# A second Strassen level inside one of the seven products of a cross-network kernel

## The chip, the cores and the metric

The kernel runs on one core of one Trainium2 chip. The metric is the device time of one execution in microseconds (us). Every kernel time below is a median of fast runs; the repeats of one kernel agree within 0.3%. Profile figures are of one execution. The traces kept for runs 1 to 4 (the first four experiments) are of another execution of the same kernel than the one quoted here; figures marked "kept trace" were counted there. The engines are named as in the profile: PE is TensorE (matmuls), PEld its weight loads, DVE is VectorE, ACT is ScalarE, SP issues the transfers.

## The reference

```python
B, Din, L = 16384, 1024, 6          # x0 [B, Din], ws [L, Din, Din], bs [L, Din], all bf16
def reference(x0, ws, bs):
    x = x0
    for l in range(L):
        proj = jnp.einsum('bd,de->be', x, ws[l]) + bs[l]
        x = x0 * proj + x
    return x
```

Each of the six layers multiplies x by a 1024x1024 matrix, and layer l+1 needs the whole result of layer l.

## The kernel before

x is kept transposed in SBUF (features on partitions). 1024 rows of the batch, called a pair, are taken through all six layers, then the next 1024: 16 pairs x 6 layers = 96 rounds, called layers here. Within a layer, one Strassen (Winograd) step cuts the product into blocks of 512: seven products of 512x512x512 instead of eight. A product is 16 matmuls of 512 columns. Block (eh, n) is output half eh (512 features) of batch half n (512 rows).

The T's are differences of blocks of x, made by DVE. The weight combinations are made by DVE in the first pair and then reloaded from memory. PSUM holds two tiles `pA` and two tiles `px`, each of two banks.

```python
rhs_of = {1: blk(xsrc, 0, 0), 2: blk(xsrc, 1, 0), 3: blk(xsrc, 1, 1),
          4: Ts[4][:], 5: Ts[1][:], 6: Ts[2][:], 7: Ts[3][:]}

def product(pid, pts, start):                    # 16 matmuls
    ...                                          # (weight tile wt, cut)
    for m in range(KH):
        for k in range(KH):
            nc.tensor.matmul(pts[m // 2][:, m % 2, :], lhsT=wt[:, k, m * P:(m + 1) * P], rhs=rhs[:, k, :],
                             start=(start and k == 0), stop=(k == KH - 1), **kw)

def evac(pts, bias_eh=None, dst=None):           # ScalarE: PSUM -> SBUF, bf16
    ...                                          # two 1024-element copies, or four 512-element ones with a bias

def final(Cb, eh, n):                            # VectorE: x_new = x0 * c + x, block by block
    c = Cb[:, :, n, :]
    nc.vector.tensor_tensor(out=c, in0=c, in1=blk(x0T, eh, n), op=MULT)
    ...                                          # (last pair, cut)
    nc.vector.tensor_tensor(out=blk(xst, eh, n), in0=c, in1=blk(xsrc, eh, n), op=ADD)

# (PSUM allocation and the first pair's weight combinations cut)
product(1, pA, True);   P1s = evac(pA)
product(5, pX, True);   P5s = evac(pX)
product(3, pX, False);  S53 = evac(pX, bias_eh=0)
product(2, pX2, True);  P2s = evac(pX2, bias_eh=0)
nc.vector.tensor_tensor(out=C1[:, :, 0, :], in0=P1s, in1=P2s, op=ADD)
final(C1, 0, 0)                                  # block (0,0): what the next layer's product 1 reads
product(6, pA, False);  U2s = evac(pA)
nc.vector.tensor_tensor(out=C1[:, :, 1, :], in0=U2s, in1=S53, op=ADD)
final(C1, 0, 1)
...                                              # T1 of the next layer
product(7, pA, False);  U3s = evac(pA, bias_eh=1)
nc.vector.tensor_tensor(out=C2[:, :, 1, :], in0=U3s, in1=P5s, op=ADD)
final(C2, 1, 1)
product(4, pA, False);  evac(pA, bias_eh=1, dst=C2[:, :, 0, :])
final(C2, 1, 0)
...                                              # T2, T3, T4 of the next layer
```

The order of the products is 1, 5, 3, 2, 6, 7, 4. A scheduler fixes the order on each engine at build time; it may depart from the order in which the code is written.

## Time and profile before

| | before |
|---|---|
| time | 2354.6 us (2354.53 to 2354.66, 2 runs) |
| PE / DVE / ACT busy | 98% / 73% / 66% |
| matmuls in the program | 10752, all of 512 columns |

The page's first part gives busy time and share of the span, its fourth part the chain of work that ended last, by engine:

```profile
PE 2312.4 (98%) x10537; PEld 1052.7 (45%) x10752; DVE 1708.6 (73%) x1464; ACT 1556.7 (66%) x2113; POOL 1.2 (0%) x5
...
PE 96%; DVE 1%; DMA 1%; issue 1%; SPq 1%; ACT 0%; another core or an unknown queue 0%; DVEq 0%
```

Matmuls overlap (the trace gives one a mean duration of 379 ns), so a busy PE is not yet a PE at its limit. What counts is the time from one start to the next. In the trace of the kernel before it is 216 ns (median of all neighbours), and 10752 x 0.216 = 2322 us of the 2353 us span. (2% of the matmul records are missing, so the page counts 10537.) The table of waits (who waited for whom: us in total, times, longest) agrees. PE is in none of its large lines; other engines wait for PE or for each other:

```profile
DVE cb L235 <- ACT ev L208: 594.2, 96, 7.9
ACT ev L205 <- PE pa L196: 230.8, 368, 14.2
ACT ev L208 <- PE px L196: 193.3, 369, 0.8
```

The timeline of one layer (start, duration, what, count, and in brackets idle time before it) shows when block (0,0) is ready:

```profile
1214.45 3.62 PE L196 MATMUL pa<-T_9079,wp 128*128 128x512 bf16 x16
...
1215.95 1.23 DVE L235 TENSOR_TENSOR cb<-ev 128x2048 bf16<-128x2048 bf16 x1 [6.43 <-ACT ev L208]
...
1217.21 1.22 DVE L214 TENSOR_TENSOR cb<-cb,x0T 128x2048 bf16<-128x2048 bf16 x1
...
1218.54 1.23 DVE L223 TENSOR_TENSOR xst<-cb,xst 128x2048 bf16<-128x2048 bf16 x1
...
1223.34 1.27 ACT L208 ACTIVATE cb<-pa,b_all 128x512 bf16<-128x512 f32 x2 [0.51 <-ACT ev L208]
...
1224.81 0.38 PE L196 MATMUL pa<-xst,wp 128*128 128x512 bf16 x1
```

Add, multiply, add for block (0,0) end at 1218.54 + 1.23 = 1219.77. The next layer's product 1 (the last line) starts at 1224.81. Block (0,0) is five microseconds early, and PE does not stop.

### The profile page before, as it was taken

To read this page: it belongs to the slowest core of one execution; us is meant where nothing else is said; L and a number is where in the kernel's file an instruction comes from. 1 tells how busy PE (TensorE), PEld (TensorE's weight loads), DVE (VectorE), ACT (ScalarE), POOL (GpSimd) and SP (SyncE) were. 2 spreads that over 40 slices of the span, in tenths; PEclk is the share of its full clock that TensorE was granted. 3 is DMA by queue.
4 is the path that set the end of the run, shared out by engine and by line. 5 is a ranking of instruction groups with operands and counts; after the bars stand their busy time and mean duration, and the time that the engine had idled before them with its cause. 6 is when DMAs were issued, how large, how long until landed. Compare 5 with 4: busy or idle time off the path is not lost.

```text
span 2352.8 us, 27562 instructions
## 1 busy us (share of the span) xinstructions
PE 2312.4 (98%) x10537; PEld 1052.7 (45%) x10752; DVE 1708.6 (73%) x1464; ACT 1556.7 (66%) x2113; POOL 1.2 (0%) x5
## 2 busy tenths in 40 slices
PE   7999999999999999999999999999999999999997
PEld 3444444444444444444444444444444444444443
DVE  5977767676777767676776767677776767777675
ACT  4666666666666666666666666666666666666665
POOL 0000000000000000000000000000000000000000
PEclk9999999999999999999999999999999999999998
DMA  7769485584956849568494774947749476594843
GB/s 226 203 210 256 152 216 196 161 253 154 228 184 171 241 154 240 171 177 235 153 259 153 178 233 152 259 152 190 221 152 260 153 198 214 155 257 152 226 153 86
DMA packets 599987, 457.96 MB, mean 195 GB/s; under 512 B 398128, under 2 KB 550704, under 8 KB 599856
## 3 DMA queue, kind: packets, MB, share of 16 engines
q1 hardware_dynamic: 599856, 456.20, 67.0%
q8 instruction: 85, 1.39, 0.2%
q14 instruction: 46, 0.38, 0.1%
HBM read 342.88 MB, written 46.14 MB: 165 GB/s over the span
## 4 chain that ended last, share of the span: by engine, by line
PE 96%; DVE 1%; DMA 1%; issue 1%; SPq 1%; ACT 0%; another core or an unknown queue 0%; DVEq 0%
PE pa L196 54%; PE px L196 42%; SPq L145 1%; DMA w_313<-in_ws_dram 0%; DMA wp<-in_ws_dram 0%; DVE cb L214 0%; DVE xst L219 0%; DVE xst L223 0%; ACT ev L208 0%; DVE cb L241 0%; DVE cb L250 0%; DVE cb L235 0%; DVE wp L128 0%; DVE T_247 L93 0%; DVE T_811 L93 0%
## 5 line engine op out<-in xcount | busy, mean ns | idle before, releaser
L196 PEld LDWEIGHTS <-wp 128*128 128x128 bf16 x10752 | 1052.7, 98 | 1283.8 <-issue 12.7
L208 ACT ACTIVATE ev<-px,b_all 128x512 bf16<-128x512 f32 x768 | 486.3, 684 | 201.3 <-PE px L196 193.3
L196 PE MATMUL px<-xst,wp 128*128 128x512 bf16 x2510 | 562.5, 379 | 2.7
L235 DVE TENSOR_TENSOR cb<-ev 128x2048 bf16<-128x2048 bf16 x96 | 117.6, 1225 | 594.2 <-ACT ev L208 594.2
L205 ACT CAST ev<-pa 128x1024 bf16<-128x1024 f32 x384 | 388.6, 1012 | 240.2 <-PE pa L196 230.8
L214 DVE TENSOR_TENSOR cb<-cb,x0T 128x2048 bf16<-128x2048 bf16 x384 | 467.8, 1221 | 6.3
L223 DVE TENSOR_TENSOR xst<-cb,xst 128x2048 bf16<-128x2048 bf16 x316 | 385.0, 1222 | 14.5
L208 ACT ACTIVATE ev<-pa,b_all 128x512 bf16<-128x512 f32 x384 | 243.1, 684 | 112.9 <-PE pa L196 108.2
L208 ACT ACTIVATE cb<-pa,b_all 128x512 bf16<-128x512 f32 x384 | 243.1, 684 | 88.4 <-ACT ev L208 48.4
L196 PE MATMUL pa<-xst,wp 128*128 128x512 bf16 x1254 | 287.3, 379 | 1.3
L205 ACT CAST ev<-px 128x1024 bf16<-128x1024 f32 x192 | 194.3, 1012 | 138.1 <-PE px L196 133.1
L241 DVE TENSOR_TENSOR cb<-ev 128x2048 bf16<-128x2048 bf16 x96 | 117.0, 1219 | 0.0
L250 DVE TENSOR_TENSOR cb<-ev 128x2048 bf16<-128x2048 bf16 x96 | 117.0, 1218 | 0.0
L196 PE MATMUL px<-x0T,wp 128*128 128x512 bf16 x501 | 112.4, 379 | 0.5
L223 DVE TENSOR_TENSOR xst<-cb,x0T 128x2048 bf16<-128x2048 bf16 x64 | 78.3, 1223 | 1.5
L196 PE MATMUL pa<-x0T,wp 128*128 128x512 bf16 x251 | 60.2, 391 | 12.9 <-DMA x0T<-in_x_dram 12.6
L130 DVE TENSOR_TENSOR wp<-wp 128x2048 bf16<-128x2048 bf16 x6 | 7.3, 1219 | 2.1 <-DMA wp<-in_ws_dram 2.1
L128 DVE TENSOR_TENSOR wp<-wp 128x2048 bf16<-128x2048 bf16 x6 | 7.3, 1219 | 0.0
L126 DVE TENSOR_TENSOR wp<-w_90,wp 128x2048 bf16<-128x2048 bf16 x1 | 1.2, 1226 | 8.2 <-DMA wp<-in_ws_dram 8.2
L93 DVE TENSOR_TENSOR T_111<-x0T 128x2048 bf16<-128x2048 bf16 x1 | 1.2, 1226 | 5.7 <-DMA x0T<-in_x_dram 5.7
L219 DVE TENSOR_TENSOR xst<-cb,xst 128x2048 bf16<-128x2048 bf16 x4 | 4.9, 1225 | 0.1
L196 PE MATMUL px<-T_247,wp 128*128 128x512 bf16 x16 | 3.6, 378 | 0.3 <-DVE T_247 L93 0.3
(783 smaller groups left out, 1858.9 us busy)
## 6 DMA issues: line engine op xcount, KB each, us to landing
wp<-Lc SPq DMA_DIRECT2D x360, 512.0 KB, 3.4
wp<-in_ws_dram SPq DMA_DIRECT2D x288, 512.0 KB, 3.7
out_dram<-x0T SPq DMA_DIRECT2D x30, 1024.0 KB, 9.8
Lc<-wp SPq DMA_DIRECT2D x24, 512.0 KB, 3.1
out_dram<-xoS SPq DMA_DIRECT2D x4, 512.0 KB, 4.7
w_90<-in_ws_dram SPq DMA_DIRECT2D x1, 512.0 KB, 4.7
x0T<-in_x_dram SPq DMA_TRANSPOSE x32, 7.3
w_130<-in_ws_dram SPq DMA_DIRECT2D x1, 512.0 KB, 5.0
```

What stands on the lines that cost most here:

```text
L128: nc.vector.tensor_tensor(out=t_[:], in0=wtiles[(0, l, 5)][:], in1=W11[:], op=SUB)
L130: nc.vector.tensor_tensor(out=t_[:], in0=W21[:], in1=wtiles[(0, l, 6)][:], op=SUB)
L145: nc.sync.dma_start_transpose(out=x0T_next[:, n], in_=x0[n * NB:(n + 1) * NB, :])
L196: nc.tensor.matmul(pts[m // 2][:, m % 2, :], lhsT=wt[:, k, m * P:(m + 1) * P], rhs=rhs[:, k, :], start=(start and k == 0), stop=(k == KH - ...
L205: nc.scalar.copy(out=dst[:, 2 * h:2 * h + 2, :], in_=pts[h][:])
L208: nc.scalar.activation(out=dst[:, m, :], in_=pts[m // 2][:, m % 2, :], func=IDENT, bias=bias_col(bias_eh, m), scale=1.0)
L214: nc.vector.tensor_tensor(out=c, in0=c, in1=blk(x0T, eh, n), op=MULT)
L219: nc.vector.tensor_tensor(out=xo_last["xfin"][:, eh, n].rearrange("r j k p -> r k j p"), in0=v4(c), in1=v4(blk(xsrc, eh, n)), op=ADD)
L223: nc.vector.tensor_tensor(out=blk(xst, eh, n), in0=c, in1=blk(xsrc, eh, n), op=ADD)
L235: nc.vector.tensor_tensor(out=C1[:, :, 0, :], in0=P1s, in1=P2s, op=ADD)
L241: nc.vector.tensor_tensor(out=C1[:, :, 1, :], in0=U2s, in1=S53, op=ADD)
L250: nc.vector.tensor_tensor(out=C2[:, :, 1, :], in0=U3s, in1=P5s, op=ADD)
```

## The change

Product 2, W21*B21, is itself cut into blocks of 256 and done with seven inner products, each of four matmuls of 256 columns. PE then has 28 half-size matmuls where it had 16 whole ones. The inner results go through PSUM to SBUF, and DVE sums them into the four quadrants of block (0,0). To hide the evacuations, the author spread the inner products over products 6 and 7.

```diff
-    ORDER = [1, 5, 3, 2, 6, 7, 4]
+    ORDER = [1, 5, 3, 6, 2, "2i", 7, 4]
+    def emit_t(B):                      # four quarter-size T's of B21 on VectorE
+        ...
+            def iproduct(i, dst, start):        # 4 matmuls of 256 columns
+                ...
-            product(2, pX2, True)
-            P2s = evac(pX2, bias_eh=0)
-            nc.vector.tensor_tensor(out=C1[:, :, 0, :], in0=P1s, in1=P2s, op=ADD)
-            final(C1, 0, 0)
-            product(6, pA, False)
-            U2s = evac(pA)
+            product(6, pA, False, (0, 1))
+            nc.scalar.copy(out=U2s[:, 0:2, :], in_=pA[0][:])
+            iproduct(1, y0[:, 0, :], True)
+            iproduct(5, y0[:, 1, :], True)
+            nc.scalar.copy(out=i15[:], in_=y0[:])
+            product(6, pA, False, (2,))
+            iproduct(2, y1[:, 0, :], True)
+            nc.scalar.copy(out=i2[:], in_=y1[:, 0, :])
+            product(6, pA, False, (3,))
+            nc.scalar.copy(out=U2s[:, 2:4, :], in_=pA[1][:])
+            ...
+            iproduct(6, y0[:, 0, :], False)     # accumulate on 1 and 5, so after their copy
+            iproduct(3, y0[:, 1, :], False)
+            nc.scalar.copy(out=i63[:], in_=y0[:])
+            ...                                 # block (0,1)
+            product(7, pA, False, (0,))
+            evac_b(U3s, pA, 1, (0,))
+            iproduct(7, y0[:, 0, :], False)
+            nc.scalar.copy(out=i7[:], in_=y0[:, 0, :])
+            product(7, pA, False, (1, 2))
+            ...
+            iproduct(4, y0[:, 0, :], False)
+            nc.scalar.copy(out=cq(1, 0), in_=q3(y0[:, 0, :]))
+            product(7, pA, False, (3,))
+            evac_b(U3s, pA, 1, (3,))
+            nc.vector.tensor_tensor(out=C11, in0=C11, in1=P1s, op=ADD)
+            final(C1, 0, 0)
             ...
             product(4, pA, False)
```

(Cut: weight handling, the bias that moves to product 1's evacuation, the four quadrant sums, the inner weight combinations in the first pair, buffer counts.)

More of the change, by code (lines that the diff above doesn't have):

```diff
@@ L42 @@
     t_pool = ctx.enter_context(tc.tile_pool(name="tp", bufs=1))
-    ev_pool = ctx.enter_context(tc.tile_pool(name="evp", bufs=7))
+    ti_pool = ctx.enter_context(tc.tile_pool(name="tip", bufs=2))
+    evi_pool = ctx.enter_context(tc.tile_pool(name="evi", bufs=1))
+    ev_pool = ctx.enter_context(tc.tile_pool(name="evp", bufs=6))
     cb_pool = ctx.enter_context(tc.tile_pool(name="cbp", bufs=2))
@@ L51 @@
     xo_pool = None
-    Lc = dram.tile([L, 4, P, KH * H], BF16, name="Lc")
-    CIDX = {5: 0, 6: 1, 7: 2, 3: 3}
+    Lc = dram.tile([L, 5, P, KH * H], BF16, name="Lc")
+    CIDX = {5: 0, 6: 1, 7: 2, 3: 3, "2i": 4}
     def w_src(l, pid):
@@ L64, in w_src @@
         return Lc[l, CIDX[pid]].rearrange("p (k e) -> p k e", k=KH)
-    ORDER = [1, 5, 3, 2, 6, 7, 4]
+    ORDER = [1, 5, 3, 6, 2, "2i", 7, 4]
+    KQ, HQ, NQ = KH // 2, H // 2, NB // 2
     all_keys = [(pr, l, pid) for pr in range(NPAIR) for l in range(L) for pid in ORDER]
@@ L99, in emit_T, with inner_w @@
                 nc.vector.tensor_tensor(out=t_[:], in0=B21, in1=Ts[2][:], op=SUB)
+    def inner_w(t):
+        v = t[:].rearrange("p q (k e) -> p q k e", k=KQ)
+        return {5: v[:, 0], 6: v[:, 1], 3: v[:, 2], 7: v[:, 3]}
+    def emit_t(B):
+        q = lambda dh, n: B[:, dh * KQ:(dh + 1) * KQ, n * NQ:(n + 1) * NQ]
+        t_ = ti_pool.tile([P, 4, KQ, NQ], BF16, name="ti")
+        t1, t3, t2, t4 = (t_[:, i] for i in range(4))
+        nc.vector.tensor_tensor(out=t1, in0=q(0, 1), in1=q(0, 0), op=SUB)
+        nc.vector.tensor_tensor(out=t3, in0=q(1, 1), in1=q(0, 1), op=SUB)
+        nc.vector.tensor_tensor(out=t2, in0=q(1, 1), in1=t1, op=SUB)
+        nc.vector.tensor_tensor(out=t4, in0=q(1, 0), in1=t2, op=SUB)
+        return {1: q(0, 0), 2: q(1, 0), 3: q(1, 1), 4: t4, 5: t1, 6: t2, 7: t3}
     combo_st = {}
@@ L130, in emit_combo @@
             nc.vector.tensor_tensor(out=t_[:], in0=W21[:], in1=wtiles[(0, l, 6)][:], op=SUB)
-        else:
-            nc.vector.tensor_tensor(out=t_[:], in0=W11[:], in1=w12[:], op=SUB)
+        elif pid == 7:
+            nc.vector.tensor_tensor(out=t_[:], in0=W11[:], in1=w12[:], op=SUB)
+        else:
+            a11, a12 = W21[:, 0:KQ, 0:HQ], W21[:, KQ:KH, 0:HQ]
+            a21, a22 = W21[:, 0:KQ, HQ:H], W21[:, KQ:KH, HQ:H]
+            s = inner_w(t_)
+            nc.vector.tensor_tensor(out=s[5], in0=a21, in1=a22, op=ADD)
+            nc.vector.tensor_tensor(out=s[6], in0=s[5], in1=a11, op=SUB)
+            nc.vector.tensor_tensor(out=s[3], in0=a12, in1=s[6], op=SUB)
+            nc.vector.tensor_tensor(out=s[7], in0=a11, in1=a21, op=SUB)
         wtiles[(0, l, pid)] = t_
@@ L150 @@
     prefetch_upto(7)
-    for pid in (5, 6, 3, 7):
+    for pid in (5, 6, 3, 7, "2i"):
         emit_combo(0, pid)
@@ L186, with weight, product @@
             combos_next = pr == 0 and l + 1 < L
-            def product(pid, pts, start):
-                key = (pr, l, pid)
-                prefetch_upto(key_pos[key] + PREF)
-                wt = wtiles.pop(key) if not (pr == 0 and pid in (1, 2, 4)) else wtiles[key]
+            wcur = {}
+            def weight(pid):
+                if pid not in wcur:
+                    key = (pr, l, pid)
+                    prefetch_upto(key_pos[key] + PREF)
+                    wcur[pid] = wtiles.pop(key) if not (pr == 0 and pid in (1, 2, 4)) else wtiles[key]
+                return wcur[pid]
+            def product(pid, pts, start, ms=range(KH)):
+                wt = weight(pid)
                 rhs = rhs_of[pid]
-                for m in range(KH):
+                for m in ms:
                     for k in range(KH):
@@ L197, in product @@
                                          start=(start and k == 0), stop=(k == KH - 1), **kw)
+            def iproduct(i, dst, start):
+                if i in (1, 2, 4):
+                    k0, e0 = {1: (0, 0), 2: (KQ, 0), 4: (KQ, HQ)}[i]
+                    wv = weight(2)[:, k0:k0 + KQ, e0:e0 + HQ]
+                else:
+                    wv = inner_w(weight("2i"))[i]
+                for m in range(KQ):
+                    for k in range(KQ):
+                        st = start and m == 0 and k == 0
+                        nc.tensor.matmul(dst[:, m * NQ:(m + 1) * NQ], lhsT=wv[:, k, m * P:(m + 1) * P], rhs=ti[i][:, k, :],
+                                         start=st, stop=(k == KQ - 1), skip_group_check=True)
             def evac(pts, bias_eh=None, dst=None):
@@ L223, in final @@
                     nc.vector.tensor_tensor(out=blk(xst, eh, n), in0=c, in1=blk(xsrc, eh, n), op=ADD)
+            ti = emit_t(rhs_of[2])
             product(1, pA, True)
-            P1s = evac(pA)
+            P1s = evac(pA, bias_eh=0)
             pX = [psX.tile([P, 2, NB], FP32, name="px") for _ in range(2)]
@@ L231 @@
             S53 = evac(pX, bias_eh=0)
-            pX2 = [psX.tile([P, 2, NB], FP32, name="px") for _ in range(2)]
-            product(2, pX2, True)
-            P2s = evac(pX2, bias_eh=0)
-            nc.vector.tensor_tensor(out=C1[:, :, 0, :], in0=P1s, in1=P2s, op=ADD)
-            final(C1, 0, 0)
+            C11 = C1[:, :, 0, :]
+            cq = lambda eh, n: C11[:, eh * KQ:(eh + 1) * KQ, n * NQ:(n + 1) * NQ]
+            q3 = lambda a: a.rearrange("p (m b) -> p m b", m=KQ)
+            y0 = psX.tile([P, 2, NB], FP32, name="px")
@@ new lines @@
+            y1 = psX.tile([P, 2, NB], FP32, name="px")
+            U2s = ev_pool.tile([P, KH, NB], BF16, name="ev")
+            i15 = evi_pool.tile([P, 2, NB], BF16, name="i15")
+            i63 = evi_pool.tile([P, 2, NB], BF16, name="i63")
+            i2 = evi_pool.tile([P, NB], BF16, name="i2")
+            i7 = evi_pool.tile([P, NB], BF16, name="i7")
+            product(6, pA, False, (0, 1))
+            nc.scalar.copy(out=U2s[:, 0:2, :], in_=pA[0][:])
+            iproduct(1, y0[:, 0, :], True)
@@ new lines @@
+            iproduct(5, y0[:, 1, :], True)
[5 more added lines that the diff above has]
+            nc.scalar.copy(out=U2s[:, 2:4, :], in_=pA[1][:])
+            nc.vector.tensor_tensor(out=cq(0, 0), in0=q3(i15[:, 0, :]), in1=q3(i2[:]), op=ADD)
+            iproduct(6, y0[:, 0, :], False)
+            iproduct(3, y0[:, 1, :], False)
@@ L237 @@
+            nc.scalar.copy(out=i63[:], in_=y0[:])
+            nc.vector.tensor_tensor(out=C1[:, :, 1, :], in0=U2s[:], in1=S53, op=ADD)
+            final(C1, 0, 1)
+            nc.vector.tensor_tensor(out=cq(0, 1), in0=q3(i63[:, 0, :]), in1=q3(i63[:, 1, :]), op=ADD)
             if combos_next:
                 emit_combo(l + 1, 5)
-            product(6, pA, False)
-            U2s = evac(pA)
-            nc.vector.tensor_tensor(out=C1[:, :, 1, :], in0=U2s, in1=S53, op=ADD)
-            final(C1, 0, 1)
+            if combos_next:
+                emit_combo(l + 1, 6)
@@ new lines, with evac_b @@
+            U3s = ev_pool.tile([P, KH, NB], BF16, name="ev")
+            def evac_b(dst, pts, eh, ms):
+                for m in ms:
+                    nc.scalar.activation(out=dst[:, m, :], in_=pts[m // 2][:, m % 2, :], func=IDENT,
+                                         bias=bias_col(eh, m), scale=1.0)
+            product(7, pA, False, (0,))
[3 more added lines that the diff above has]
+            product(7, pA, False, (1, 2))
@@ L243 @@
+            evac_b(U3s, pA, 1, (1, 2))
+            nc.vector.tensor_tensor(out=cq(1, 1), in0=q3(i7[:]), in1=q3(i15[:, 1, :]), op=ADD)
+            iproduct(4, y0[:, 0, :], False)
[4 more added lines that the diff above has]
+            final(C1, 0, 0)
             if nxt_src is not None:
@@ L245 @@
                 emit_T(nxt_src, Tn)
-            if combos_next:
-                emit_combo(l + 1, 6)
-            product(7, pA, False)
-            U3s = evac(pA, bias_eh=1)
-            nc.vector.tensor_tensor(out=C2[:, :, 1, :], in0=U3s, in1=P5s, op=ADD)
+            nc.vector.tensor_tensor(out=C2[:, :, 1, :], in0=U3s[:], in1=P5s, op=ADD)
             final(C2, 1, 1)
@@ L253 @@
                 emit_combo(l + 1, 3)
+                emit_combo(l + 1, "2i")
             product(4, pA, False)
```

## The prediction

> **What bounds the kernel now.** TensorE. In the page's busy table PE is at 98%, VectorE (DVE) 73%, ScalarE (ACT) 66%; the chain of waits gives PE 96% of the span; the table of waits shows no recurring PE wait. The timeline in mid-kernel gives a product of 16 matmuls every 3.456 us: 216 ns for 512 columns. The Trainium skill ("TensorE: Matmul & The Clock Gate", "Wait — 56ns, not 53.3ns?") states N/2.4 GHz + 2.5 ns = 215.8 ns; the trace agrees. 10752 x 0.216 = 2322 us; some 32 us are fill and drain.
>
> **Removed.** Per layer and pair (96 of them) 16 matmuls of 512 columns become 28 of 256. By the same formula 256 columns cost an estimated 109 ns (weight loads took 98 ns, so I expect them to stay hidden). 3.456 us become 3.06: 0.40 us a layer, 38 us in all. This is the whole possible gain, 1.6%.
>
> **Added.** DVE: seven quarter-size operations (four for the T's, three for quadrants), an estimated 0.34 us each, scaled from 1.135 us spacing of 2048-element ones: 2.4 us a layer, 228 us in all, DVE some 78-80% busy. ACT: the removed evacuation was four at 0.684; added are two 1024-element copies (1.01) and three 512-element ones. P1's evacuation turns from two copies into four biased ones. A 512 copy is an estimated 0.59 us (the ScalarE page of the skill, "What ACT_TABLE_LOAD costs": immediates cost 0.833 ns per element plus a constant; the trace's 1012 ns for 1024 elements leaves 159). ACT rises by about 1.6 us a layer, to about 68%. Neither engine is full; what matters is latency.
>
> **Moved: the step that decides.** Before, block (0,0) of the next x, which the next layer's product 1 reads, was finished early: product 2 ran fourth, and two products followed. Now it needs all seven inner products, and the last (4) comes almost at the end: only the rest of product 7 and product 4, some 20 matmuls or 4.3 us plus small stalls, run between its end and the next product 1. In that time: semaphore 0.2, ACT finishing queued evacuations and the quadrant copy 1.1, then DVE add, multiply, add, with another add put between by the instruction order (4 x 1.135, plus latencies 0.3): about 6.1 us. So PE waits about 1.5 us at product 1 in layers whose successor is in the same pair: 80 of 96, about 125 us.
>
> Second, PSUM reuse: inner product 7 accumulates into the bank read by the evacuation of 6 and 3, queued on ACT behind a 1.01 us copy, with only five outer matmuls between: about 0.4 us of PE wait; the finely cut product 7 waits for its evacuations, about 0.2-0.3. Together 0.6-0.7 us x 96 = 60-65 us.
>
> Sum: 2354.6 - 38 + 125 + 62, plus about 12 in the first pair (weight combinations lengthen DVE's queue) = 2516 us.
>
> **Predicted: 2516 us, 8 in 10 within 2475 to 2555.** Faster by over 2%: 0.02 (PE's count forbids it); within 2%: 0.06; slower: 0.92.
>
> **What shows it.** PE busy falls to 91-93%, with a new line in the waits: PE at product 1 on DVE's final add, 80 times, 1.3-1.8 us; PE at the 256-column matmuls on ACT, 96 times, 0.3-0.5 us. Matmul spacing at 256 columns of 109 ns. The chain of waits moves from PE 96% to a mix with DVE at 15-25%. Clock stays at 1.0.
>
> **What would make it wrong.** 256-column matmuls slower than 109 ns (each 10 ns costs 27 us); slower small ACT or DVE operations; on the other side, quicker handovers (0.1 us in the chain is 8 us) or PE running other work into the wait. If product 1's wait is absent, the time would be near 2390.

## The result, and the profile after

| | before | after |
|---|---|---|
| time, us | 2354.6 | 2495.5 (2495.10 and 2495.95) |
| ratio | | 1.0599, 95% interval 1.0568 to 1.0629 |
| PE / DVE / ACT busy | 98 / 73 / 66% | 94 / 78 / 68% |
| matmul start to start, 512 columns | 216 ns | 216 ns |
| matmul start to start, 256 columns | | 109 ns |

A ratio is the mean time of one kernel's fast runs over that of the other's fast runs of the same rounds, so it is not quite the ratio of the medians. The range held, and the point was 20 us (0.8%) too high. The record marks the outputs of the five experiments below as correct.

The page and the table of waits of the changed kernel:

```profile
PE 2339.4 (94%) x11904; PEld 1159.0 (46%) x11904; DVE 1934.9 (78%) x2160; ACT 1696.8 (68%) x2401; POOL 1.1 (0%) x5
...
PE 83%; ACT 11%; DMA 2%; DVE 2%; issue 1%; SPq 0%; DVEq 0%
```

```profile
PE pa L228 <- ACT cb L252: 93.2, 71, 1.3
...
PE pa L228 <- DVE xst L267: 17.8, 5, 5.4
```

PE now waits ahead of product 1 in all 80 layers that follow another one in the same pair. But the table puts 71 of these waits down to ACT's evacuation of product 4 (`cb`, L252), only 5 to DVE's final add of the new x (`xst`, L267), and 4 to DMAs. The prediction had named DVE. The timeline of one such layer shows why the label can't settle it:

```profile
1196.59 0.60 PE L240 MATMUL px<-ti,wp 128*128 128x256 bf16 x4
...
1197.52 0.58 ACT L322 CAST cb<-px 128x512 bf16<-128x512 f32 x1
...
1198.13 1.22 DVE L325 TENSOR_TENSOR cb<-cb,ev 128x2048 bf16<-128x2048 bf16 x1 [0.26 <-ACT cb L322]
1198.54 3.19 PE L228 MATMUL pa<-T_9645,wp 128*128 128x512 bf16 x14
...
1199.39 1.22 DVE L258 TENSOR_TENSOR cb<-cb,x0T 128x2048 bf16<-128x2048 bf16 x1
1200.08 1.26 ACT L252 ACTIVATE cb<-pa,b_all 128x512 bf16<-128x512 f32 x2 [0.66 <-PE pa L228]
1200.54 1.22 DVE L330 TENSOR_TENSOR cb<-ev 128x2048 bf16<-128x2048 bf16 x1
1201.67 1.22 DVE L267 TENSOR_TENSOR xst<-cb,xst 128x2048 bf16<-128x2048 bf16 x1
1201.76 1.26 ACT L252 ACTIVATE cb<-pa,b_all 128x512 bf16<-128x512 f32 x2 [0.41 <-PE pa L228]
...
1203.03 3.61 PE L228 MATMUL pa<-xst,wp 128*128 128x512 bf16 x16 [1.31 <-ACT cb L252]
```

From top to bottom: the last inner product; its copy; DVE's add (L325) and multiply (L258) for block (0,0); ACT's evacuation of the first `pA` tile of product 4; an add for another block (L330); the final add of (0,0) (L267). This ends at 1201.67 + 1.22 = 1202.89. ACT's evacuation of the second `pA` tile ends at 1201.76 + 1.26 = 1203.02, and product 1 starts at 1203.03. Both candidates end within 0.15 us, and a table that names the one that came last names ACT.

From the matmul starts in the trace (the time from one start to the next, less 216 or 109 ns for the first of the two), every PE wait can be added up:

| where PE waits | each | times | sum |
|---|---|---|---|
| ahead of product 1 | 1.476 us (median) | 80 | 129.3 us |
| ahead of inner product 7 | 0.239 | 96 | 22.9 |
| within the interleaved products 7 and 4 | 0.146 and 0.071 | 96 each | 20.8 |
| saved by smaller matmuls: 16 x 0.216 - 28 x 0.109 | -0.404 | 96 | -38.8 |

The sum is +134 us. Matmuls at half clock in the first pair (last section) add about 6 us, and the tail after the last matmul starts is 18.8 us long instead of 16.2, while the lead before the first is 0.9 us shorter; the waits of the kernel before were 1.7 us. That accounts for the 140.5 us between the two spans to within 1 us.

What the table does not tell is what releases product 1. The trace as a whole does. In all 80 layers product 1 starts 145 to 147 ns after the final add of block (0,0) ends, also in the five of the first pair, where ACT had finished with product 4 at least 1.2 us before. In the other 75, ACT had ended 6 to 14 ns before the start, while the PSUM waits of the same trace (the second and third row) end 50 to 53 ns after the ACT evacuation of the tile that PE writes next, 288 times out of 288. And the evacuation that the label points to empties the second `pA` tile; the first eight matmuls of product 1 write the first one, which ACT had emptied at least 1.68 us earlier. The experiments test the same by changing the kernel.

### The profile page after: what moved, and what is told of

It is laid out like the page before. It is cut to its first block, busy times and chain, and to the rows that moved or that the text cites. A ratio compares the mean times of both kernels' runs of the same rounds, so it can differ in the third digit from the quotient of the medians.

```text
span 2493.3 us, 31597 instructions
## 1 busy us (share of the span) xinstructions
PE 2339.4 (94%) x11904; PEld 1159.0 (46%) x11904; DVE 1934.9 (78%) x2160; ACT 1696.8 (68%) x2401; POOL 1.1 (0%) x5
## 4 chain that ended last, share of the span: by engine, by line
PE 83%; ACT 11%; DMA 2%; DVE 2%; issue 1%; SPq 0%; DVEq 0%
PE pa L228 48%; PE px L228 26%; PE px L240 9%; ACT cb L252 4%; ACT ev L296 3%; DMA x0T<-xst 1%; DVE cb L258 1%; DMA wp<-Lc 1%; DMA out_dram<-x0T 1%; DVE xst L267 0%; DMA x0T<-in_x_dram 0%; DVE cb L330 0%; DVE cb L325 0%; DVE cb L301 0%; ACT ev L312 0%
## 5 line engine op out<-in xcount | busy, mean ns | idle before, releaser
L228 PEld LDWEIGHTS <-wp 128*128 128x128 bf16 x9216 | 896.6, 98 | 1158.9 <-issue 170.1
L258 DVE TENSOR_TENSOR cb<-cb,x0T 128x2048 bf16<-128x2048 bf16 x384 | 466.9, 1220 | 2.6
L252 ACT ACTIVATE ev<-pa,b_all 128x512 bf16<-128x512 f32 x384 | 242.7, 683 | 223.3 <-PE pa L228 222.9
L267 DVE TENSOR_TENSOR xst<-cb,xst 128x2048 bf16<-128x2048 bf16 x316 | 383.7, 1219 | 0.0
L240 PEld LDWEIGHTS <-wp 128*128 128x128 bf16 x2688 | 262.4, 98 | 156.4 <-issue 34.6
L312 ACT ACTIVATE ev<-pa,b_all 128x512 bf16<-128x512 f32 x384 | 253.8, 686 | 108.6 <-PE pa L228 108.6
L252 ACT ACTIVATE ev<-px,b_all 128x512 bf16<-128x512 f32 x384 | 242.8, 683 | 113.1 <-PE px L228 113.1
L252 ACT ACTIVATE cb<-pa,b_all 128x512 bf16<-128x512 f32 x384 | 242.8, 683 | 102.7 <-PE pa L228 102.7
L228 PE MATMUL px<-xst,wp 128*128 128x512 bf16 x1280 | 289.3, 379 | 0.0
L240 PE MATMUL px<-ti,wp 128*128 128x256 bf16 x1536 | 230.2, 272 | 7.5 <-DVE ti L112 0.3
L301 DVE TENSOR_TENSOR cb<-ev 128x2048 bf16<-128x2048 bf16 x96 | 117.5, 1224 | 68.3 <-ACT ev L296 68.3
L240 PE MATMUL px<-xst,wp 128*128 128x256 bf16 x960 | 144.0, 273 | 0.0
L325 DVE TENSOR_TENSOR cb<-cb,ev 128x2048 bf16<-128x2048 bf16 x96 | 117.6, 1225 | 21.6 <-ACT cb L322 20.2
L288 ACT CAST ev<-pa 128x1024 bf16<-128x1024 f32 x96 | 97.2, 1012 | 44.3 <-PE pa L228 44.3
L330 DVE TENSOR_TENSOR cb<-ev 128x2048 bf16<-128x2048 bf16 x96 | 117.0, 1219 | 0.2
L296 ACT CAST ev<-pa 128x1024 bf16<-128x1024 f32 x96 | 97.2, 1012 | 26.7 <-PE pa L228 26.7
L267 DVE TENSOR_TENSOR xst<-cb,x0T 128x2048 bf16<-128x2048 bf16 x64 | 78.0, 1219 | 0.0
L322 ACT CAST cb<-px 128x512 bf16<-128x512 f32 x96 | 56.1, 585 | 0.0
```

The source lines that it names most:

```text
L240: nc.tensor.matmul(dst[:, m * NQ:(m + 1) * NQ], lhsT=wv[:, k, m * P:(m + 1) * P], rhs=ti[i][:, k, :], start=st, stop=(k == KQ - 1), skip_g ...
L252: nc.scalar.activation(out=dst[:, m, :], in_=pts[m // 2][:, m % 2, :], func=IDENT, bias=bias_col(bias_eh, m), scale=1.0)
L288: nc.scalar.copy(out=U2s[:, 0:2, :], in_=pA[0][:])
L296: nc.scalar.copy(out=U2s[:, 2:4, :], in_=pA[1][:])
L301: nc.vector.tensor_tensor(out=C1[:, :, 1, :], in0=U2s[:], in1=S53, op=ADD)
L312: nc.scalar.activation(out=dst[:, m, :], in_=pts[m // 2][:, m % 2, :], func=IDENT, bias=bias_col(eh, m), scale=1.0)
```

## The experiments

Theory A is that of the prediction: product 1 waits for DVE to finish block (0,0), which is late because it now needs the last inner product. Theory B is what the table of waits says: product 1 waits for ACT to empty PSUM after product 4. A third candidate was that the second level itself costs PE or the small operations more than it saves.

### 1. One VectorE operation out of the chain

```diff
-            nc.vector.tensor_tensor(out=C2[:, :, 1, :], in0=U3s[:], in1=P5s, op=ADD)
+            a22 = nc.vector.tensor_tensor(out=C2[:, :, 1, :], in0=U3s[:], in1=P5s, op=ADD)
+            # f00: the final add of block (0,0); NoSync orders, and adds no semaphore
+            if f00 is not None:
+                tc.add_manual_dep(a22.ins, f00.ins.name,
+                    mybir.DependencyInfo(mybir.DependencyClass.NoSync, mybir.DependencyReason.DATA), ...)
```

> The changed kernel with one VectorE instruction moved: the add for block (1,1) is held behind the final add of block (0,0), without any semaphore, so one operation of 1.13 us leaves the chain that ends in block (0,0). Work, ScalarE and PSUM are untouched. Theory A (product 1 of the next layer waits for block (0,0) on VectorE): the wait ahead of product 1 falls from 1.48 us to about 0.4 us in 80 layers, total about 2410 us (2400 to 2420). Theory B (product 1 waits for ScalarE to empty the PSUM tile of product 4, as the table of waits names it): wait and time stay, about 2495 us.

Measured: 2421.8 us, ratio 1.0288 to the kernel before (interval 1.0273 to 1.0303). The wait ahead of product 1 fell from 1.476 to 0.535 us (median). Timeline of that run:

```profile
1166.07 1.23 DVE L258 TENSOR_TENSOR cb<-cb,x0T 128x2048 bf16<-128x2048 bf16 x1
...
1167.40 1.23 DVE L267 TENSOR_TENSOR xst<-cb,xst 128x2048 bf16<-128x2048 bf16 x1
1168.43 1.26 ACT L252 ACTIVATE cb<-pa,b_all 128x512 bf16<-128x512 f32 x2 [0.41 <-PE pa L228]
1168.54 1.22 DVE L330 TENSOR_TENSOR cb<-ev 128x2048 bf16<-128x2048 bf16 x1
...
1168.77 3.61 PE L228 MATMUL pa<-xst,wp 128*128 128x512 bf16 x15 [0.37 <-DVE xst L267]
```

Product 1 starts at 1168.77, 0.14 us after the final add ends (1168.63) and 0.92 us before ACT is through with product 4 (1169.69). Theory B falls: ACT's work is the same, and product 1 does not wait for it. The time is 12 us above the expectation, just outside its range. The multiply and the final add now follow each other directly, and the second starts 1.33 us after the first instead of 1.135: taking out an operation of 1.135 us brought 0.94 us.

### 2. The kernel before, with product 2 moved to late

No second level; only the place of product 2 changes, and with it that of the block (0,0) work and of T1.

```diff
-    ORDER = [1, 5, 3, 2, 6, 7, 4]
+    ORDER = [1, 5, 3, 6, 7, 2, 4]
             product(7, pA, False)
             U3s = evac(pA, bias_eh=1)
+            product(2, pX2, True);  P2s = evac(pX2, bias_eh=0)      # moved from behind product 3
+            nc.vector.tensor_tensor(out=C1[:, :, 0, :], in0=P1s, in1=P2s, op=ADD)
+            final(C1, 0, 0)                                          # then the add of (1,1), then T1
```

> The kernel before, no second level at all, product 2 moved from fourth place to between products 7 and 4; same number of matmuls, evacuations and VectorE operations. Theory A: block (0,0) is again ready late, product 1 waits about 3 us in 80 layers, total about 2600 us (2560 to 2640). Theory B: nothing about PSUM of product 4 changes, so 2355 us. If the cost came from the second level itself (256 columns, more small operations), 2355 us as well.

Measured: 2714.9 us, ratio 1.1535 (interval 1.1516 to 1.1554).

```profile
243.18 1.27 ACT L208 ACTIVATE cb<-pa,b_all 128x512 bf16<-128x512 f32 x2 [0.41 <-PE pa L196]
...
244.83 1.22 DVE L223 TENSOR_TENSOR xst<-cb,xst 128x2048 bf16<-128x2048 bf16 x1
...
246.20 3.61 PE L196 MATMUL pa<-xst,wp 128*128 128x512 bf16 x15 [3.06 <-DVE xst L223]
```

ACT had emptied product 4 at 244.45, and product 1 starts at 246.20, 0.15 us after the final add (246.05). The place alone, without a single 256-column matmul, makes PE wait 3.2 us in each such layer (267 us in 80). This is again theory A, and it shows that lateness alone, without a second level, is enough for this wait. The time is 115 us above the expectation, a miss: after 56 of the 73 waits of 3.1 or 3.2 us, several matmuls of product 1 start 427 ns apart instead of 216 (half clock), which adds some 96 us (kept trace; gaps of 431 or 432 ns, two whole steps with one record missing, are not counted).

### 3. Inner products early, VectorE order left to the scheduler

The seven inner products move up to where product 2 stood and mix with product 6 only. Product 7 is whole again. Inner product 4 gets the free PSUM bank, so it no longer waits for the copy of 7, at the price of one more quarter-size add. The T's of the next pair are now made in the same places as those within a pair.

```diff
+            iproduct(1, y0[:, 0, :], True);  iproduct(5, y0[:, 1, :], True)     # straight after product 3
+            product(6, pA, False, (0,))
+            iproduct(2, y1[:, 0, :], True);  iproduct(4, y1[:, 1, :], True)
+            product(6, pA, False, (1,))
+            iproduct(6, y0[:, 0, :], False); iproduct(3, y0[:, 1, :], False)
+            product(6, pA, False, (2, 3))
+            iproduct(7, y0[:, 0, :], False)
+            ...                                        # copies and sums, then block (0,0), (0,1)
+            product(7, pA, False);  U3s = evac(pA, bias_eh=1)
-            nxt_src = xst if l + 1 < L else None
+            nxt_src = xst if l + 1 < L else (None if last_pair else x0T_next)
```

> Second level kept, its seven products moved up to where product 2 stood, interleaved with product 6 alone, product 7 in one piece; inner product 4 gets a PSUM bank of its own and two quarter T's are made before T3 and T4. The order on VectorE is left to the scheduler, which puts the chain of block (0,1) and the block (1,1) work among that of (0,0). Theory A: product 1 still waits, about 2.6 us in 80 layers, total about 2530 us (2500 to 2560), while the waits of the 256-column matmuls on ScalarE are gone. Theory B: the wait goes, since ScalarE has less to do before product 4 ends; about 2330 us.

Measured: 2613.4 us, ratio 1.1097 (interval 1.1081 to 1.1114). Product 1 waits 2.756 us (median, 225 us in all). The waits ahead of the 256-column matmuls are gone. Theory B predicted the opposite. The inner products come earlier and product 1 waits longer, since the scheduler spread the work of (0,1) and (1,1) among that of (0,0):

```profile
1196.65 1.22 DVE L333 TENSOR_TENSOR cb<-cb,ev 128x2048 bf16<-128x2048 bf16 x1
1197.78 1.22 DVE L292 TENSOR_TENSOR xst<-cb,xst 128x2048 bf16<-128x2048 bf16 x1
1198.92 1.22 DVE L283 TENSOR_TENSOR cb<-cb,x0T 128x2048 bf16<-128x2048 bf16 x1
1200.05 1.22 DVE L346 TENSOR_TENSOR cb<-ev 128x2048 bf16<-128x2048 bf16 x1
1201.19 1.22 DVE L292 TENSOR_TENSOR xst<-cb,xst 128x2048 bf16<-128x2048 bf16 x1
```

The add, multiply and final add of (0,0) are the first, third and fifth line; the final add of (0,1) and the add of (1,1) stand between them. Again the time is above the expectation, by 83 us. In the kept trace matmuls at half clock add some 65 us of this. The stretches of the trace with the granted clock show it (the column behind POOL):

```profile
1199.50:1202.50 3.00, 0.46 (x3) 0.00 (x0) 3.00 (x4) 1.35 (x3) 0.00 (x0) 0.99 1.02 403
1202.50:1205.50 3.00, 2.95 (x8) 1.06 (x9) 3.00 (x3) 0.00 (x0) 0.00 (x0) 0.50 1.10 363
```

In the first stretch PE waits (busy 0.46 of 3.00 us). In the second, product 1 runs, at a clock of 0.50 (1.00 is full speed).

### 4. The same, VectorE held in program order

```diff
+    # a wrapper around VectorE: every instruction gets a NoSync order edge to the one before it
-            nc.vector.tensor_tensor(...)
+            vec.tensor_tensor(...)
```

> As the run before it, and VectorE's instructions are held in the order in which the kernel writes them (no semaphores added): quadrants, then block (0,0), then (0,1), then the rest; the next pair's T's are written in the same places as those within a pair. Theory A: product 1 no longer waits; in the first pair the weight combinations still cost some 15 to 20 us; total about 2345 us (2335 to 2360), that is 0.4% below the kernel before. Theory B: no difference from the run before it.

Measured: 2397.6 us, ratio 1.0186 (interval 1.0171 to 1.0201, so the verdict at 2% is unclear): 216 us less than the run before it, with the same work (TensorE's order differs a little too, as the scheduler follows). As A expects, product 1 no longer waits. But the time is 52 us above the expectation, a miss. PE now waits about 0.27 us ahead of product 3 and of inner product 1 in most layers, 54 us in all (kept trace), about the size of the miss. The timeline shows the wait at product 3 (the last line):

```profile
1187.79 1.23 DVE L38 TENSOR_TENSOR xst<-cb,xst 128x2048 bf16<-128x2048 bf16 x1
...
1189.12 1.23 DVE L38 TENSOR_TENSOR T<-xst 128x2048 bf16<-128x2048 bf16 x1
1190.26 1.22 DVE L38 TENSOR_TENSOR cb<-ev 128x2048 bf16<-128x2048 bf16 x1
...
1190.49 3.61 PE L253 MATMUL px<-T,wp 128*128 128x512 bf16 x16
...
1191.52 1.23 DVE L38 TENSOR_TENSOR cb<-cb,x0T 128x2048 bf16<-128x2048 bf16 x1
...
1192.85 1.23 DVE L38 TENSOR_TENSOR xst<-cb,xst 128x2048 bf16<-128x2048 bf16 x1
...
1194.22 3.61 PE L253 MATMUL px<-xst,wp 128*128 128x512 bf16 x15
```

DVE starts an operation that reads the result of the one just before it 1.25 to 1.33 us after that one's start (here 1187.79 to 1189.12), and an independent one after 1.135 us (1189.12 to 1190.26 takes 1.14). The last three DVE lines are such a row (add, multiply and final add of block (1,1)), and product 3, which reads that block, starts 0.14 us after it ends (1194.08). The order as written has some nine such pairs in a layer, and DVE is 85% busy.

### 5. A fitted version

The inner products are packed tighter (1, 5, a quarter of product 6, 2, 4, 6, 3, then six matmuls of product 6, then 7). On DVE the two blocks' operations alternate, so that a result is rarely read by the next operation. From the second pair on, ACT is held in program order too. In the first pair, where DVE also makes the weight combinations, product 2 stays plain.

```diff
-            final(C1, 0, 0)
-            final(C1, 0, 1)
+                mul(C1, 0, 0)
+                mul(C1, 0, 1)
+                fadd(C1, 0, 0)
+                fadd(C1, 0, 1)
+                vec.tensor_tensor(out=C2[:, :, 1, :], in0=U3s, in1=P5s, op=ADD)
+                ...                      # T1, then (1,1) and (1,0) in the same way
```

> Second level in 15 of the 16 pairs, the first pair as in the kernel before (its VectorE also makes the weight combinations). The seven inner products run straight after product 3 among the first ten matmuls of product 6, so the evacuation of 7 ends some 7.5 us ahead of the next product 1; VectorE is held in an order in which an operation rarely follows the one whose result it reads. Laid out with the durations and gaps that the runs so far show, no wait of TensorE is left inside a layer and block (0,0) is ready some 0.6 us early. If theory A and the 109 ns matmul are the whole story: 90 layers x 0.40 us = 35 us below the kernel before, about 2322 us (2315 to 2335). If the second level carries another cost of its own on TensorE: 2354 us or more.

Measured: 2329.5 us, ratio to the kernel before 0.9896 (interval 0.9879 to 0.9912), 24.3 us less. This is the fastest kernel, though its gain is inside 2%. The page, and the timeline around product 1:

```profile
PE 2293.2 (98%) x11832; PEld 1157.2 (50%) x11832; DVE 1954.2 (84%) x2208; ACT 1663.4 (71%) x2293; POOL 1.1 (0%) x5
```

```profile
1208.86 2.35 DVE L38 TENSOR_TENSOR cb<-cb,x0T 128x2048 bf16<-128x2048 bf16 x2
...
1211.13 2.35 DVE L38 TENSOR_TENSOR xst<-cb,xst 128x2048 bf16<-128x2048 bf16 x2
...
1213.04 3.62 PE L255 MATMUL pa<-xst,wp 128*128 128x512 bf16 x16
1213.24 1.27 ACT L38 ACTIVATE cb<-pa,b_all 128x512 bf16<-128x512 f32 x2 [0.41 <-PE pa L255]
```

Two adds in 2.35 us: the first, of block (0,0), ends some 0.7 us ahead of product 1 (my estimate: 1211.13 + 1.22 = 1212.35), and product 1 has no idle time before it, while ACT is still emptying product 4. Of the possible 36.4 us (90 layers x 0.404), 5.8 us are lost to a wait of 0.065 us ahead of inner product 7, about 4 us to more waits in the first pair and at its end, and 2.3 us to lead and tail (the tail is 19.2 us, before 16.2). The saving of the second level on PE is thus real, and most of it can be had.

## Why the prediction was right, point by point

- **What bounds the kernel: right.** PE at 216 ns a matmul; no recurring wait before.
- **The gain of 0.40 us a layer: right.** The estimated 109 ns for 256 columns is what the trace shows (109.0 ns). Run 5 shows that most of the gain can be had.
- **The small operations: right in kind.** The copy of 512 elements was put at 0.59 us and measures 0.585. DVE's quarter-size operation takes 0.42 us but starts every 0.335 (estimated: 0.34). DVE went to 78% and ACT to 68%, as predicted.
- **The wait at product 1: right, and shown by runs 1 to 4.** Predicted were about 1.5 us in 80 layers, 125 us; measured 1.476 us in the median and 129.3 us in all. The 6.1 us from the last inner product to product 1 measure 6.0 (its four matmuls end at about 1197.03, that is 1196.59 + 4 x 0.109; product 1 starts at 1203.03).
- **The waits on PSUM: right in mechanism, mis-sized.** The step was "about 0.4 us of PE wait" for inner product 7, and "together 0.6-0.7 us x 96 = 60-65 us". It measures 0.239 + 0.146 + 0.071 = 0.456 us, 43.7 us. This is 18 of the 20 us by which the point was too high. The waits at product 1 (129.3 us, where the sum had 125 + 12) were another 8 us below it; half clock and the longer tail took back some 6. That these waits come from evacuations was read from the order, from the steady 50 to 53 ns after an ACT evacuation, and from their disappearance in run 3; no run of their own tests them.
- **The 12 us of the first pair: about right.** Its five waits are 18.6 us, against 5 x 1.476 = 7.4 had they been like the others: 11 us more, plus about 6 us of half clock that was not foreseen.
- **What the profile would show: partly wrong.** It was to be "PE at product 1 on DVE's final add, 80 times", and "the chain of waits moves from PE 96% to a mix with DVE at 15-25%". The table names DVE 5 times, ACT 71 times and DMAs 4 times, and the chain has ACT 11%, DVE 2%. PE busy is 94%, predicted 91-93%. The cause was right, its signature was not: two things ended within 0.15 us, and the view names the later. In run 1, where they lie apart, it names DVE.

## What to carry to other kernels

Count what a rewrite saves on the bounding engine, then ask when the results that it now delivers later are first read: here 0.40 us a layer was saved, and a block that had been ready five microseconds early came 1.5 us late. When a wait has two candidates that end almost together, don't take the profile's label for the cause. Look which of the two the start follows at a constant distance in every layer, then move one of them by a microsecond and see whether the wait follows. When the bounding engine reads what another engine makes, the order of that engine's instructions can matter as much as their number: runs 3 and 4 do the same work and differ by 216 us.

## What the Trainium skill lacked or had wrong

- "TensorE: Matmul & The Clock Gate", section "Wait — 56ns, not 53.3ns?": N / 2.4 GHz + 2.5 ns agrees with the traces, at 512 columns (216 ns against 215.8) and at 256 (109.0 against 109.2). The section "Back-to-back issue gap" of the same page says that at large N this formula over-counts, and gives about 131 ns for sustained N = 512. In these traces, thousands of load-and-multiply pairs in a row have a median of 216 ns, and none of the kernels comes near 131.
- The same page, section "What's actually happening", has the half clock come after at least one idle window of about 3.4 us, and its section "Why this matters for your kernels" warns of gaps over about 3 us. Here shorter waits were enough: waits of about 2.8 us ahead of product 1 were followed by matmuls at 427 ns in 37 of 76 cases (run 3, kept trace), those of 3.1 and 3.2 us in 56 of 73 (run 2, kept trace), those of 1.5 us in none of 75 (the changed kernel). It cost some 65 us in run 3 and some 96 us in run 2.
- "VectorE: DVE Perf Modes", section "The perf-mode tier table", gives 1224 ns for a bf16 `tensor_tensor` of 2048 elements, and the traces agree (1220). In its section "The DRAIN you can't avoid" it finds that a semaphore after each operation costs nothing extra, on copies. It has no figure for an operation that reads the result of the one just before: here that starts 1.25 to 1.33 us after it, an independent one after 1.135 us. With some nine such pairs in a layer this is the likely cause of most of the 52 us by which run 4 missed; run 5, which has few of them, lies within 8 us of its expectation, though it also changes the order on PE and ACT.
- None of the pages that I read says that a wait with two candidates that end together can be put down to the wrong one. Here it was 71 of 80.
